# Gate weights in row blocks on two queues, six gate steps abreast, one transpose a tile

## The chip, the cores and the metric

The kernel runs on one core of a Trainium2 chip. Its five engines run side by side and wait for each other through semaphores: TensorE (PE, matmuls; its weight loads are listed as PEld), VectorE (DVE), ScalarE (ACT), GpSimd (POOL) and SyncE (SP, which here only issues DMAs; ACT and POOL issue some too). Matmuls write PSUM, a small memory that ACT and DVE must empty; everything else lies in SBUF, which has 128 partitions. The metric is device time of one execution in microseconds, as the median of three runs.

## The reference

The input x has 2048 tokens of 448 features. It is normalised to xn and goes through a linear recurrence with complex diagonal coefficients (an S5 layer) and, on the other side, through a gated feed-forward block; the two results are multiplied and x is added.

```python
def _B_ref(x, w_gate, w_up, w_down):
    g = jnp.einsum("bsd,df->bsf", x, w_gate)      # 448 -> 1792
    u = jnp.einsum("bsd,df->bsf", x, w_up)
    h = _sigmoid(g) * u
    return jnp.einsum("bsf,fd->bsd", h, w_down)   # 1792 -> 448

xn = _layernorm(x)
s = _A_ref(xn, ...)      # h[t] = Lam_bar * h[t-1] + B_bar xn[t];  2 Re(C h) + xn * Dskip
return x + s * _silu(_B_ref(xn, B_w_gate, B_w_up, B_w_down))
```

Weights, x and the result are bf16.

## The kernel before

**Tiling.** The tokens are cut into 16 tiles of 128 and 4 chunks of 512 (4 tiles). Features lie on partitions for the matmuls, so each tile of xn is transposed into `xnT`. For chunk 0 PE transposes (`pe_transpose`, L511) and ACT and DVE copy the result out of PSUM; for chunks 1 to 3 SP issues DMA transposes (`dma_transpose`, L533), two for a tile: one of four blocks of 128 columns and one of three.

448 is seven times 64. The gate and up weights `wG` and `wU` are therefore held as 7 slots of 64 rows on each half of the partitions: the lower 64 partitions hold the first 896 of the 1792 columns, the upper 64 the other 896. One gate or up step (`gu_mm`, L720) is one block m of 128 columns of each half; it makes 7 pairs of 64-row matmuls (L730, L731), and the two of a pair run side by side on the two halves of the PE array. A chunk has 7 gate and 7 up steps. `xnT` has seven slots too. Slot s of it holds features 64 s to 64 s + 127 (the last wraps round), so its lower half goes with weight slot s and its upper half with weight slot s + 1.

**PSUM.** There are three slots `gu` of two banks each, and two single banks `acc`. A step fills one `gu` slot with 2 x 512 columns. After a gate step ACT takes Tanh of it (`gu_evac`, L748; sigmoid is made from Tanh) and after an up step DVE multiplies (L751). In chunk 0 the gate steps come first, then all up steps. Gate step 3 of chunk 0 uses the two `acc` banks (L743).

**Order.** Every operation is entered with `add` into a plan (class `Plan`). PE's operations keep the order in which they are entered, and so do all DMAs of one queue; ACT, DVE and POOL are ordered by a planner from costs and due times that are written in the code. The `land` arguments are such times; they delay nothing on the chip. At the very start DVE too keeps the entered order (`pl.seq`). Eight semaphores serve the DMAs of SP and ACT in turn, so a DMA is issued only after the eighth before it has landed.

**The start.** SP and ACT load x tiles 0 to 3, then the gate weights in column blocks (L361, L392 to L397): m 0, 1 of the lower half on SP (224 KB) and of the upper half on ACT, then m 2, 3 and m 4 to 6 of the lower half on SP with x tiles 4 to 7 between them, and m 2 to 6 of the upper half in one piece on ACT (560 KB). Four up blocks and `dbc` follow on SP (L412 to L416), then the transposes of B (`b_load`), the tile transposes of chunk 1, `wd`, C (`c_load`), and x tiles 8 to 15 (L1050).

PE first runs matmuls on zeros (`warm_mm`), transposes tiles 0 and 1, and then runs `columns` (L556): small matmuls that turn three rows of parameters (`vrow`, loaded by POOL's queue into `hF`) into columns. From these POOL makes the decay and the angle, and `tables` (L591) makes cosine and sine tables; its first product, iota times angle (L596), is made by ACT. Then PE runs

```python
gu_mm(0, "g", 0, slots0[0], 0, 1, True)       # L1015: step 0, tile 0
gu_mm(0, "g", 0, slots0[0], 1, 2, False)      # step 0, tile 1
gu_mm(0, "g", 1, slots0[1], 0, 2, False)      # step 1, tiles 0, 1
pe_transpose(2, one_bank(0, "DVE"))
pe_transpose(3, one_bank(1, "DVE"))
```

then tiles 2 and 3 of steps 0 and 1, then the steps 2 to 6 with all four tiles, the seven up steps, the products with B (`b_phase`, L777), and so on chunk by chunk, with the down products (L930) and the output products (L959) of earlier chunks between. The recurrence itself is a scan on DVE (L869, L901); its result `hT` (L886, L916) feeds L959.

`norm` (L482) writes xn into one of 8 buffers of 512 columns (the last 64 repeat the first 64, copied by POOL at L493), `skip_row` (L496) makes xn times Dskip into `xd`.

Of the kernel before, what the change touches and what calls it, by code (L numbers as in the profile page):

```python
# [18 lines left out]
D = 448  # L19
F = 1792  # L20
P = 128
# [8 lines left out]
HEAD_DMA = 17  # L30
# [216 lines left out]
def kernel(  # L247
# [39 lines left out]
    NXN = 8  # L287
    xn = [sbt(f"xn{i}", [512]) for i in range(NXN)]
    xnT_raw = [sbt(f"xnT{i}", [7 * L]) for i in range(3)]
    xnT = [flat(t[:], 7, L) for t in xnT_raw]  # L290
    hF_raw = [sbt(f"hF{i}", [FT * L]) for i in range(2)]
# [30 lines left out]
    vrow = hF_raw[0][0:3, 0:448]  # L322
# [38 lines left out]
    BLK = {"g": [(0, 2), (2, 7), (2, 4), (4, 7)], "u": [(0, 3), (3, 7)]}  # L361

    def load_w(eng, k, half, b, r=(), rate=105e3, land=0.0):
        m0, m1 = BLK[k][b]
        ps = slice(half * H, half * H + H)
        c0 = half * 896
        load(eng, [("w", k, half, m) for m in range(m0, m1)], H * 7 * (m1 - m0) * P * 2,
             wgt[k][ps, :, m0 * P:m1 * P],
             wsrc[k][:, c0 + m0 * P:c0 + m1 * P].rearrange("(s p) f -> p s f", p=H), cost=0.65, r=r, rate=rate, land=land)

    def load_wd(h):
        fs = slice(h * 7, h * 7 + 7)
        load("SP", ("wd", h), F * D, wd[:, fs, :], B_w_down.rearrange("(ft p) d -> p ft d", p=P)[:, fs, :],
             rate=400e3, land=41.0 + 2.2 * h)
# [17 lines left out]
    load_w("SP", "g", 0, 0, rate=115e3)  # L392
    load_w("ACT", "g", 1, 0, rate=115e3)
    load_w("SP", "g", 0, 2, rate=400e3, land=9.4)
    load_w("ACT", "g", 1, 1, rate=400e3, land=11.8)
    load_x(4, 2, land=10.8)
    load_w("SP", "g", 0, 3, rate=400e3, land=12.4)  # L397
    load_x(6, 2, land=13.4)
# [13 lines left out]
    load_w("SP", "u", 0, 0, rate=400e3, land=14.8)  # L412
    load_w("SP", "u", 1, 0, rate=400e3, land=16.6)
    load("SP", "dbc", P * D * 2, dbc[:], A_Dskip.unsqueeze(0).to_broadcast((P, D)), rate=400e3, land=17.2)
    load_w("SP", "u", 0, 1, rate=400e3, land=19.2)
    load_w("SP", "u", 1, 1, rate=400e3, land=21.2)  # L416

# [64 lines left out]
    def norm(t):  # L482
        b = t % NXN
        if t < TPC:
            add("DVE", 0.42, lambda: V.tensor_scalar(out=xn[b][:, 0:448], in0=x_all[:, t, :],
                                                     scalar1=meanf[:, t, :], scalar2=rsd[:, t, :],
                                                     op0=ALU.subtract, op1=ALU.mult),
                r=[("x", t), ("mf", t), ("rs", t)], w=[("xn", b)])
        else:
# [3 lines left out]
            add("POOL", 0.2, lambda: G.tensor_copy(out=xn[b][:, 448:512], in_=xn[b][:, 0:64]),  # L493
                r=[("xn", b)], w=[("xnw", b)])

    def skip_row(t):  # L496
        b, q = t % NXN, t % NXD
        add("DVE", dve2(448), lambda: V.tensor_tensor(out=xd[q][:], in0=xn[b][:, 0:448], in1=dbc[:], op=ALU.mult),
            r=[("xn", b), "dbc"], w=[("xd", q)])
# [11 lines left out]
    def pe_transpose(t, parts):  # L511
        b, js = t % NXN, slice(t * P, t * P + P)
# [5 lines left out]
        def f():  # L518
            for s in range(6):
                T.transpose(tp[s], xn[b][:, s * H:s * H + P], ident[:, :])  # L520
            T.transpose(tp[6][0:H, :], xn[b][:, 384:448], ident[:, :])
            T.transpose(tp[6][H:P, :], xn[b][:, 0:H], ident[:, :])
        add("PE", 0.46, f, r=[("xn", b), "ident"], w=[p[2] for p in parts])
# [9 lines left out]
    def dma_transpose(t):  # L533
# [4 lines left out]
        tload([k + ("a",)], xnT[c % 3][:, 0:7:2, js], xn[b][:], P * 1024, r=[("xn", b), ("xnw", b)] + al)  # L538
        tload([k + ("b",)], xnT[c % 3][:, 1:6:2, js], xn[b][:, 64:448], P * 768, r=[("xn", b)] + al)
# [48 lines left out]
    def silu_table():  # L588
        add("ACT", 1.3, lambda: A.preload_act_table_set("silu_and_others"), r=[("sd", t) for t in range(4)] + [("xnT", 0, 2, "a")], w=["silutab"])

    def tables():  # L591
        turn = C("turn")
        for pt in range(4):
            vk, nk = ("v", pt), ("nu", pt)
            v, nu = v_t[:, pt, :], nu_t[:, pt, :]
            add("ACT", 0.61, lambda v=v, pt=pt: A.activation(v, iota[:, 0:NTAB], ACT.Copy, scale=turn[:, pt:pt + 1]),  # L596
                r=[("wv", 0), "turn", "silutab"], w=[vk])
# [28 lines left out]
        gate([("vrow", q) for q in range(3)], [("hF", 0, m) for m in range(7)])  # L626
# [38 lines left out]
    def b_load():  # L665
        for i, m in enumerate((A_B_re, A_B_im)):
            tload([("bT", i)], bT[:, 0:3, i, :], m[:, 0:384], D * 768, land=24.0 + 1.4 * i)
            tload([("bT3", i)], bT[:, 3:4, i, :], m[:, 320:448], D * 256, land=24.4 + 1.8 * i)
# [10 lines left out]
    def c_load():  # L679
        for i, m in enumerate((A_C_re, A_C_im)):  # L680
            tload([("rC", i)], rawC[:, i, 0:3, :], m[:, 0:384], D * 768, land=44.6 + 2.5 * i)
            tload([("rC3", i)], rawC[:, i, 3:4, :], m[:, 320:448], D * 256, land=45.4 + 2.4 * i)
# [37 lines left out]
    def gu_mm(c, k, m, a, lo, hi, first):  # L720
        x = xnT[c % 3]
        bank, keys = ([gu[a][:, 0, :], gu[a][:, 1, :]], [("gu", a)]) if a is not None else (
            [acc[0][:], acc[1][:]], [("acc", 0), ("acc", 1)])
# [4 lines left out]
        def f():  # L728
            for s in range(7):
                T.matmul(bank[0][:, ts], lhsT=w_[0:H, s, ms], rhs=x[0:H, s, ts], start=(s == 0), stop=(s == 6))  # L730
                T.matmul(bank[1][:, ts], lhsT=w_[H:P, (s + 1) % 7, ms], rhs=x[H:P, s, ts],  # L731
                         start=(s == 0), stop=(s == 6))
# [319 lines left out]
    for i in range(4, 13):  # L1052
        gu_step(0, i)
# [82 lines left out]
```

## Time and profile before

| | |
|---|---|
| median of three runs | 185.8 us (185.35 to 186.23) |
| the profiled execution | 186.07 us |
| its span, first to last instruction | 184.3 us |
| granted TensorE clock | 1.00 |
| DVE busy, 40 to 140 us | 97.6 of 100 us |
| read from HBM, written | 6.77 MB, 1.84 MB |

A line of the order of time reads: start, duration, engine, line, operation, what it writes and reads, the shape, the count, and in brackets how long the engine stood idle before it and what ended that. A line of the waits reads: who waited for whom, total time, number of times, longest. In the lines by stretches of time the figures are the busy time of PE, PEld, DVE, ACT and POOL with their counts, then the granted clock, the busy share of the DMA engines, and GB/s. Matmuls overlap, so a busy PE is not a PE at full rate; the starts of successive matmuls tell the rate.

DMAs are told by the time from issue to landing:

```profile
wU<-in_B_w_up_dram SPq DMA_DIRECT2D x2, 448.0 KB, 10.9
...
wG<-in_B_w_gate_dram ACTq DMA_DIRECT2D x1, 560.0 KB, 9.9
wG<-in_B_w_gate_dram SPq DMA_DIRECT2D x2, 224.0 KB, 6.6
...
xnT<-xn SPq DMA_TRANSPOSE x24, 2.4
...
wG<-in_B_w_gate_dram ACTq DMA_DIRECT2D x1, 224.0 KB, 5.5
```

### The profile page before, as it was taken

The numbers are of one execution on the slowest core, as the hardware profiler recorded it, in microseconds if no ns is written. First come the engines' busy times: TensorE is split into PE (matmuls) and PEld (weight loads), VectorE is DVE, ScalarE is ACT, GpSimd is POOL, SyncE is SP. The second block draws the span as 40 slices with busy tenths as digits, with TensorE's granted clock in tenths as the row PEclk, the third lists the DMA queues.
The fourth block names the chain that finished last, engine by engine and source line by source line (L and its number), as shares of the span: only waits on it lengthen the run. The fifth ranks groups of instructions, "written<-read, shape, count | busy, mean of one in ns | idle before, by whom it ended". The sixth has DMA issues, their size and how long they took to land.

```text
span 184.3 us, 3593 instructions
## 1 busy us (share of the span) xinstructions
PE 177.8 (96%) x1395; PEld 88.9 (48%) x1402; DVE 166.1 (90%) x296; ACT 95.7 (52%) x155; POOL 32.5 (18%) x95
## 2 busy tenths in 40 slices
PE   7899999999999999999999999999999999999992
PEld 2664455474554444454554444454555444455551
DVE  3856999599998989999999999999999998999963
ACT  3666999877699897666130452439120523411100
POOL 7355328000047247710000000000000000000000
PEclk9999999999999999999999999999999999999999
DMA  5999994479910340243000000002000000001120
GB/s 139 249 201 211 154 188 88 84 204 279 251 38 20 80 82 21 50 82 71 0 2 0 28 1 0 4 0 75 0 4 0 25 25 5 27 0 50 56 96 28
DMA packets 29826, 13.44 MB, mean 73 GB/s; under 512 B 19760, under 2 KB 29808, under 8 KB 29808
## 3 DMA queue, kind: packets, MB, share of 16 engines
q1 hardware_dynamic: 28496, 12.16, 30.8%
q10 hardware_dynamic: 1216, 1.03, 2.4%
q8 instruction: 11, 0.18, 0.4%
q14 instruction: 7, 0.06, 0.1%
q0 software_dynamic: 96, 0.00, 0.0%
HBM read 6.77 MB, written 1.84 MB: 47 GB/s over the span
## 4 chain that ended last, share of the span: by engine, by line
PE 86%; DMA 7%; ACT 2%; DVE 2%; issue 1%; SPq 1%; DVEq 0%
PE gu L730 39%; PE gu L930 14%; PE acc L959 11%; PE acc L930 9%; PE gu L802 8%; DMA x_all<-in_A_x_dram 7%; PE gu L788 2%; PE acc L805 2%; PE gu L731 1%; ACT hT L596 1%; DVE bst L428 1%; SPq L354 1%; ACT xn L490 1%; ACT hF L748 0%; DVE o_t L975 0%
## 5 line engine op out<-in xcount | busy, mean ns | idle before, releaser
L730 PE MATMUL gu<-xnT,wU 64*128 64x512 bf16 x196 | 45.9, 376 | 0.3 <-ACT hF L748 0.3
L731 PE MATMUL gu<-xnT,wU 64*128 64x512 bf16 x196 | 45.9, 376 | 0.0
L731 PE MATMUL gu<-xnT,wG 64*128 64x512 bf16 (+2 forms) x238 | 44.8, 332 | 0.1
L730 PE MATMUL gu<-xnT,wG 64*128 64x512 bf16 (+2 forms) x238 | 44.8, 332 | 0.1
L748 ACT ACTIVATE sig<-gu 128x1024 f32<-128x1024 f32 x21 | 21.3, 1021 | 23.0 <-PE gu L731 23.0
L930 PEld LDWEIGHTS <-hF 128*128 128x128 bf16 x224 | 21.9, 98 | 20.7 <-issue 0.2
L730 PEld LDWEIGHTS <-wG 64*128 64x128 bf16 x245 | 21.3, 94 | 16.1
L730 PEld LDWEIGHTS <-wU 64*128 64x128 bf16 x196 | 18.4, 94 | 21.7
L751 DVE SCALAR_TENSOR_TENSOR hF<-sig,gu 128x1024 bf16<-128x1024 f32 x21 | 25.5, 1214 | 2.9 <-PE gu L731 2.5
L930 PE MATMUL gu<-wd,hF 128*128 128x448 bf16 x140 | 28.0, 352 | 0.0
L731 PEld LDWEIGHTS <-wG 64*128 64x128 bf16 x245 | 21.2, 94 | 4.4 <-DMA wG<-in_B_w_gate_dram 0.4
L869 DVE TENSOR_TENSOR_SCAN wv<-c_r,st,z 128x512 bf16<-128x512 f32 x18 | 22.9, 1275 | 0.0
L959 PE MATMUL acc<-cT,hT 128*128 128x448 bf16 (+1 forms) x112 | 22.6, 346 | 0.0
L936 ACT ACTIVATE g_t<-gu 128x448 bf16<-128x448 f32 x10 | 5.4, 541 | 28.0 <-PE gu L930 18.9
L731 PEld LDWEIGHTS <-wU 64*128 64x128 bf16 x196 | 18.2, 94 | 1.1 <-issue 1.0
L816 ACT CAST bus<-gu 128x1024 bf16<-128x1024 f32 x12 | 12.0, 1011 | 12.8 <-PE gu L788 12.3
L930 PE MATMUL acc<-wd,hF 128*128 128x448 bf16 x84 | 16.9, 352 | 0.0
L959 PEld LDWEIGHTS <-hT 128*128 128x128 bf16 x119 | 11.5, 98 | 10.1 <-issue 0.4
L802 PE MATMUL gu<-xnT,bT 128*128 128x512 bf16 x65 | 15.3, 379 | 0.4
L428 DVE BATCH_NORM_STATS2 bst<-x_all 128x6 f32<-128x448 bf16 x12 | 7.0, 613 | 5.1 <-DMA x_all<-in_A_x_dram 5.1
L822 ACT CAST bus<-acc 64x256 bf16<-64x256 f32 (+1 forms) x24 | 8.7, 369 | 4.8 <-PE acc L805 4.5
L971 DVE TENSOR_TENSOR o_t<-acc,xd 128x448 bf16<-128x448 f32 (+1 forms) x16 | 9.6, 601 | 1.5 <-PE acc L959 1.4
(146 smaller groups left out, 241.9 us busy)
## 6 DMA issues: line engine op xcount, KB each, us to landing
out_dram<-o_t SPq DMA_DIRECT2D x15, 112.0 KB, 1.7
wd<-in_B_w_down_dram SPq DMA_DIRECT2D x2, 784.0 KB, 5.7
wU<-in_B_w_up_dram SPq DMA_DIRECT2D x2, 448.0 KB, 10.9
x_all<-in_A_x_dram SPq DMA_DIRECT2D x2, 448.0 KB, 4.9
wU<-in_B_w_up_dram SPq DMA_DIRECT2D x2, 336.0 KB, 11.6
wG<-in_B_w_gate_dram ACTq DMA_DIRECT2D x1, 560.0 KB, 9.9
wG<-in_B_w_gate_dram SPq DMA_DIRECT2D x2, 224.0 KB, 6.6
x_all<-in_A_x_dram SPq DMA_DIRECT2D x2, 224.0 KB, 10.2
```

The source lines that it names most:

```text
L428: add("DVE", 0.6, lambda: V.bn_stats(out=bst[b][:], in_=x_all[:, t, :]), r=[("x", t)] + ([("xnT", 0, 3, "a")] if 3 < t < 8 else []), w=[(" ...
L730: T.matmul(bank[0][:, ts], lhsT=w_[0:H, s, ms], rhs=x[0:H, s, ts], start=(s == 0), stop=(s == 6))
L731: T.matmul(bank[1][:, ts], lhsT=w_[H:P, (s + 1) % 7, ms], rhs=x[H:P, s, ts], start=(s == 0), stop=(s == 6))
L748: add("ACT", act(1024), lambda: A.activation(th, gu[a][:], ACT.Tanh, scale=0.5), r=[("gu", a)], w=[tk])
L751: add("DVE", dve1(1024), lambda: V.scalar_tensor_tensor(out=ho, in0=th, scalar=1.0, in1=gu[a][:], op0=ALU.add, op1=ALU.mult), r=[("gu", a) ...
L802: T.matmul(gu[slots[pt]][:, i, :], lhsT=bT[:, kt, i, pt * P:pt * P + P], rhs=x[:, 2 * kt, :], start=(first and kt == 0), stop=(not first a ...
L816: add("ACT", act(1024), lambda: A.copy(out=bus[u][:], in_=gu[slots[pt]][:]), r=key(pt), w=[("bus", u)])
L822: add("ACT", 0.36, lambda ns=ns, d=d, q=q, l=l, i=i: A.copy(out=bus[u][d, l, ns], in_=acc[a3[i]][q, 0:256]), r=[("acc", a3[i])] + ([("bus" ...
L869: dve(1.194, lambda k=k: V.tensor_tensor_scan(out=wv[:, k, :], data0=rb, data1=z[:, k, :], initial=(st[pt][:, k, :] if c else 0.0), op0=AL ...
L930: T.matmul(d, lhsT=hF[c % 2][:, m, h, js], rhs=wd[:, ft, :], start=(ft == 0), stop=(ft == FT - 1))
L959: T.matmul(y, lhsT=hT[c % 2][:, hm, js], rhs=cT[:, cm, c0:c1], start=(i == 0 and not on_pe), stop=(i == 6))
L971: add("DVE", dve1(n), lambda od=od, y=y, c0=c0, c1=c1: V.tensor_tensor(out=od, in0=y, in1=xq[:, c0:c1], op=ALU.add), r=[key, ("xd", q)], w ...
```

## The change

The gate weights are loaded in blocks of whole row slots, (0, 1, 2), (3, 4) and (5, 6), all 896 columns of a half at once: the lower half on SP, the upper half on ACT, three each. `xnT` gets another order of slots (`SL`), so that both matmuls of a pair use the same weight slot. Six gate steps of chunk 0 on tiles 0 and 1 advance together: all six on slots 0 and 1 (tile 0, then tile 1), then on slot 2, then on slots 3 and 4, then on 5 and 6; two steps share one `gu` slot. Tiles 2 and 3 of the six steps follow, and step 6 as before. ACT's Tanh takes two steps for two tiles at a time. `columns` comes after slots 3 and 4. Its rows `vrow` lie in `wU` now, so the first up block is issued after it. x tiles 4 to 7 come as one load, x tiles 8 to 15 are issued after the transposes of B. A tile of chunks 1 to 3 is transposed by one DMA of seven blocks; its xn is 896 columns wide (the row twice), and POOL copies 448 columns instead of 64. There are 4 such buffers; chunk 0 uses `xd` instead. The first product of the tables is made by POOL instead of ACT.

```diff
-    NXN = 8
-    xn = [sbt(f"xn{i}", [512]) for i in range(NXN)]
+    NXN = 4
+    xn = [sbt(f"xn{i}", [2 * D]) for i in range(NXN)]
+    SL = [4 * s % 7 for s in range(7)]
-    vrow = hF_raw[0][0:3, 0:448]
+    vrow = wgt["u"][0:3, 0, 0:448]
...
-    load_w("SP", "g", 0, 0, rate=115e3)
-    load_w("ACT", "g", 1, 0, rate=115e3)
-    load_w("SP", "g", 0, 2, rate=400e3, land=9.4)
-    load_w("ACT", "g", 1, 1, rate=400e3, land=11.8)
-    load_x(4, 2, land=10.8)
-    load_w("SP", "g", 0, 3, rate=400e3, land=12.4)
-    load_x(6, 2, land=13.4)
+    for b, land in ((0, 6.2), (1, 7.8), (2, 9.4)):
+        load_w("SP", "g", 0, b, land)
+        load_w("ACT", "g", 1, b, land)
+    load_x(4, 4, rate=400e3, land=11.5)
...
-            add("POOL", 0.2, lambda: G.tensor_copy(out=xn[b][:, 448:512], in_=xn[b][:, 0:64]),
+            add("POOL", 0.5, lambda: G.tensor_copy(out=xn[b][:, D:2 * D], in_=xn[b][:, 0:D]),
...
-        tload([k + ("a",)], xnT[c % 3][:, 0:7:2, js], xn[b][:], P * 1024, r=[("xn", b), ("xnw", b)] + al)
-        tload([k + ("b",)], xnT[c % 3][:, 1:6:2, js], xn[b][:, 64:448], P * 768, r=[("xn", b)] + al)
+        tload([k + ("a",), k + ("b",)], xnT[c % 3][:, :, js], xn[b][:], P * 1792, r=[("xn", b), ("xnw", b)] + al)
...
-            add("ACT", 0.61, lambda v=v, pt=pt: A.activation(v, iota[:, 0:NTAB], ACT.Copy, scale=turn[:, pt:pt + 1]),
-                r=[("wv", 0), "turn", "silutab"], w=[vk])
+            add("POOL", 0.8, lambda v=v, pt=pt: G.tensor_scalar(out=v, in0=iota[:, 0:NTAB], scalar1=turn[:, pt:pt + 1],
+                                                                scalar2=None, op0=ALU.mult),
+                r=[("wv", 0), "turn"], w=[vk])
...
+    def gu_part(c, k, m, dst, key, lo, hi, s0, s1, opens, first):
...
+            for s in range(s0, s1):
+                u = (s + 6) % 7
+                T.matmul(dst[0], lhsT=w_[0:H, s, ms], rhs=x[0:H, SL[s], ts], start=(s == 0 and opens), stop=(s == 6),
+                         skip_group_check=not opens or s1 < 7)
+                T.matmul(dst[1], lhsT=w_[H:P, s, ms], rhs=x[H:P, SL[u], ts], start=(s == 0 and opens), stop=(s == 6),
+                         skip_group_check=not opens or s1 < 7)
...
+    def two_steps(i, a, lo):
+        ts = slice(lo * P, lo * P + 256)
+        add("ACT", act(1024), lambda: A.activation(hF[1][:, 2 * i:2 * i + 2, :, ts],
+                                                  gu[a][:].rearrange("p h (m t) -> p m h t", m=2), ACT.Tanh, scale=0.5),
+            r=[("gu", a), "silutab"], w=[("hF", 1, 2 * i), ("hF", 1, 2 * i + 1)])
+
+    def pair_part(m, lo, hi, s0, s1, a, opens, first=False):
+        o = 256 * (m % 2) + P * (lo % 2)
+        n = (hi - lo) * P
+        gu_part(0, "g", m, [gu[a][:, i, o:o + n] for i in range(2)], [("gu", a)], lo, hi, s0, s1, opens, first)
...
+    for t in range(2):
+        for m in range(6):
+            pair_part(m, t, t + 1, 0, 2, slots0[m // 2], t == 0 and m % 2 == 0, t == 0 and m == 0)
+    for s0, s1 in ((2, 3), (3, 5)):
+        for m in range(6):
+            pair_part(m, 0, 2, s0, s1, slots0[m // 2], False)
     columns(0)
+    load_u("SP", 0, 0, 14.0, w=[("vrow", k) for k in range(3)])
+    load_u("SP", 1, 0, 15.0)
+    load_u("SP", 0, 1, 17.0)
+    load_u("SP", 1, 1, 19.0)
...
+    for m in range(2):
+        pair_part(m, 0, 2, 5, 7, slots0[m // 2], False)
     pe_transpose(2, one_bank(0, "DVE"))
     pe_transpose(3, one_bank(1, "DVE"))
     silu_table()
     pl.seq = False
...
+    two_steps(0, slots0[0], 0)
+    for m in range(2, 6):
+        pair_part(m, 0, 2, 5, 7, slots0[m // 2], False, m == 2)
+        if m % 2:
+            two_steps(m // 2, slots0[m // 2], 0)
+    for m in range(6):
+        pair_part(m, 2, 4, 0, 7, slots0[m // 2], True)
+        if m % 2:
+            two_steps(m // 2, slots0[m // 2], 2)
     b_load()
+    load_x(8, 4, rate=400e3, land=24.0)
+    load_x(12, 4, rate=400e3, land=25.0)
```

## The prediction

> **What bounds the kernel now.** I read the table of engines first, then the chain of waits, then TensorE's (PE's) own waits, and last the order of time from 5 to 21 us on PE.
>
> ```profile
> span 184.3 us, 3593 instructions
> ...
> PE 177.8 (96%) x1395; PEld 88.9 (48%) x1402; DVE 166.1 (90%) x296; ACT 95.7 (52%) x155; POOL 32.5 (18%) x95
> ...
> PE 86%; DMA 7%; ACT 2%; DVE 2%; issue 1%; SPq 1%; DVEq 0%
> ...
> PE acc L561 <- DMA hF<-in_A_Lambda_re_dram: 0.5, 1, 0.5
> ...
> PEld L731 <- DMA wG<-in_B_w_gate_dram: 0.4, 1, 0.4
> ...
> PE gu L730 <- ACT hF L748: 0.3, 1, 0.3
> ```
>
> PE holds 86% of the chain that ended last, and its list of waits is short. From the first up step at 20.39 to 179.9 us I found no gap on PE over 0.25 us. So the kernel is PE's work laid end to end, and its time moves only if the point moves at which PE begins the up steps, or if a new hole opens. DVE is 98% busy from 40 to 140 us, but it finishes ahead of PE's need: the last part of hT of chunk 3 (L886) ends at 170.4 and its first reader (L959) starts at 172.5; for the earlier chunks the lead is 4.9 us or more. A shift of about one us is inside that.
>
> So the change is priced between 7.00 us, where PE takes up `columns`, and 20.39 us, where the first up step starts.
>
> ```profile
> 7.00 0.21 PE L561 MATMUL acc<-ident,hF 3*128 3x3 bf16 x3 [0.54 <-DMA hF<-in_A_Lambda_re_dram]
> ...
> 7.26 0.23 PE L730 MATMUL gu<-xnT,wG 64*128 64x128 bf16 x1
> ...
> 8.71 0.27 PE L730 MATMUL gu<-xnT,wG 64*128 64x256 bf16 x1
> ...
> 10.32 0.21 PE L730 MATMUL gu<-xnT,wG 64*128 64x128 bf16 x1
> ...
> 11.88 0.38 PE L730 MATMUL gu<-xnT,wG 64*128 64x512 bf16 x1
> 12.35 0.39 PE L731 MATMUL gu<-xnT,wG 64*128 64x512 bf16 x1
> ...
> 20.39 0.37 PE L730 MATMUL gu<-xnT,wU 64*128 64x512 bf16 x1 [0.32 <-ACT hF L748]
> ```
>
> These 13.39 us hold the gate steps, the transposes of tiles 2 and 3, and three holes: 0.17 before 10.32 (the copy of tile 3), 0.26 at 11.88 (a gate block not landed), 0.48 before 20.39 (a PSUM slot that ACT had not emptied). Together 0.91 us. The rate of the loads is in these stretches (the last column is GB/s):
>
> ```profile
> 3.50:4.50 1.00, 1.00 (x4) 0.35 (x3) 0.96 (x4) 0.30 (x1) 0.94 (x8) 1.00 0.65 146
> 4.50:5.50 1.00, 0.66 (x9) 0.43 (x7) 0.89 (x5) 0.30 (x1) 0.19 (x1) 1.00 1.03 274
> 5.50:6.50 1.00, 0.96 (x13) 0.56 (x10) 0.86 (x3) 0.59 (x2) 0.00 (x0) 1.00 1.13 298
> ...
> 7.00:8.00 1.00, 1.00 (x33) 0.96 (x34) 0.78 (x3) 0.55 (x3) 0.39 (x2) 1.00 1.07 209
> ...
> 40.00:42.00 2.00, 2.00 (x21) 0.85 (x18) 1.90 (x3) 1.14 (x2) 0.00 (x0) 1.00 1.08 375
> ```
>
> While blocks for both partition halves are in flight (4.5 to 6.5) the queues move 274 to 298 GB/s; with one half alone (7 to 8, ACT's 560 KB block) 209; wd, which spans all 128 partitions, 375.
>
> **Part 1, the start of the gate steps.** The first block is now three row slots for each half: 64 x 3 x 1792 B = 344 KB, 688 KB for the pair. All six steps need both, so PE starts when the later one has landed; call this T0. I count 40 KB of the x tiles as still to come at 3.5 us. Late end: at the rates of before, 146 + 274 + 298 = 718 KB are moved at 6.5, so the mean arrival of 728 KB is about 6.55. The lag of the last part behind the mean comes from the old first pair: 459 + 40 KB are through at 4.5 + (499 - 146)/274 = 5.8, but ACT's block, issued at 1.70, took 5.5 and landed at 7.2, a lag of 1.4. That gives T0 = 7.95. Early end: T0 can't be before tile 0's xnT is copied, 5.85 + 0.36 = 6.2. I take 6.8: 330 GB/s from 3.5 on (between 298 for pieces of 512 B and 375 for wd's of 896 B; the new pieces are 1792 B, and the weak second at 3.5, with a DMA share of 0.65, has fewer pieces to describe), 728/330 = 2.2, so 5.7, and a lag of 1.1.
>
> **Part 2, PE's work from T0 to the first up step.** A pair of 128 columns costs 0.0557 (28 of them from 10.32 to 11.88), of 256 columns 0.11, of 512 columns 0.2155. Slots 0, 1 on tiles 0 and 1 apart: 24 x 0.0557 = 1.34. Slot 2: 6 x 0.11 = 0.66. Slots 3, 4: 1.32. `columns`, moved in here: 0.26. Slots 5, 6 of steps 0, 1: 0.44. Transposes of tiles 2, 3 with their transitions, 8.82 to 10.32 less the hole of 0.17: 1.33. Slots 5, 6 of steps 2 to 5: 0.88. Tiles 2, 3: 42 x 0.11 = 4.62. Step 6: 7 x 0.2155 = 1.51. Sum 12.36. One hole is new: the copy of tile 3 (0.62 on DVE, after transposes and tile 2's copy) ends about 2.1 after the transposes start, PE is there after 1.33 + 0.88 less transitions: 0.0 to 0.3, I take 0.15. So the first up step starts at 6.8 + 12.5 = 19.3 instead of 20.39: a gain of 1.1. Bounds: 6.2 + 12.36 = 18.6 (gain 1.8) and 7.95 + 12.66 = 20.6 (a loss of 0.2).
>
> The cover of this sum: the second pair (459 KB) must land by T0 + 2.0, the third by T0 + 3.6. At 330 GB/s they come 1.4 and 2.8 after T0, so they cost nothing; without that cover see the first rival. The three PSUM slots now hold two steps each for half the tokens. ACT empties slot 0 in 1.02 (the row of Tanh) while PE has 1.33 + 0.88 of other work, slots 1 and 2 have 1.5 and 3 us more: nothing. The 0.48 hole goes, as four 0.62 copies of the tables leave ACT. Against a gain stands the third load on ACT's queue: it waits for an x tile that landed by 3.9, ahead of ACT's first Sqrt at 4.05; that Sqrt may slip 0 to 0.3, covered by 0.5 between tile 0's copy and T0.
>
> **Part 3, what moves behind it.** The four up blocks wait for `columns`, since vrow now lies in wU; PE reads it at about 10.1. SP stands until then with everything behind it. The up load then runs 11.5 to 11.5 + 1606/222 = 18.7 (222 GB/s was its rate at 18 to 20). Steps 0 to 2 have theirs at 14.6 + 1.4 = 16.0 against 19.3 needed, the rest at 20.1 against 23.8. Hidden by 3 us. The tables' products on POOL: between 0.57 (IOTA on the same 513 elements) and 1.05 (its pow) each, done by 17 us; before, ACT gave the last at 22.5. Nothing for PE. POOL's copy of the row grows from 64 to 448 columns; 0.24 and, for 192 columns, 0.35 are in the trace, so about 0.57, twelve times: POOL is 18% busy.
>
> One transpose a tile: the four-block one took 1.21 to issue and the three-block one 1.25, so width did not set it. Four at 1.25 (I take this) or, at the other end, 2.5 for both together. They come after x of chunks 2, 3: the B transposes end some 4.5 after the last up block, as before, at 23.7; x takes 918/375 = 2.5; then 4 x 1.25 to 4 x 2.5, and 2.4 to landing: 33.6 to 38.6. PE wants tiles 6 and 7 at 38.2 - 1.1 = 37.1. So 0 or, at worst, 1.5; I take 0. Later loads of wd and C only come earlier.
>
> **Sum.** 184.3 - 1.1 = 183.2 of span. The profiled execution took 186.07, 1.77 more than its span and 0.27 over the median 185.8; 184.97 in its terms is 184.7 against the median. Its own range by the bounds is 184.0 to 186.0.
>
> **Rivals.** *The halves don't add up.* With row blocks the two queues move no more than one half's 209 GB/s. Then the first pair is through at 3.5 + 728/209 = 7.0, plus 1.4 is 8.4; the second lands at 10.6, the third at 12.8, and after the third PE still has 0.44 + 1.33 + 0.88 + 0.15 + 4.62 + 1.51 = 8.95: up steps from 21.8, a loss of 1.4, 187.2. It decides from a third pair landing after 20.39 - 8.95 = 11.4. For it: over 11 to 19 us, where single halves follow each other, the rate stays near 222. Against it: 274 to 298 with both halves in flight. *Late but without holes.* The lag of 1.4 stays and nothing else: 20.5, 185.9, no change that can be told. For it: the landing of the old pair. *The transposes eat it.* Chunk 1 waits 1.5: 186.2; against it, the two equal issue times.
>
> On the first rival the Trainium skill takes a side. "SBUF — State Buffer", section "Can I just issue two DMAs to hit both halves?", says no: two transfers at once, one to each partition half, were only 6% faster than one. The 298 against 209 GB/s here disagree with it, by 43%; by the rule (1.06 x 209 = 222 GB/s) the third pair would land at about 12.4 and the kernel would be some 1 us slower, by the measured rows it is 1.1 faster. I go by the rows.
>
> **How the numbers follow.** A measurement can tell about 0.5%, 0.9 us, from no change. Forecast 0.55, of it 0.50 faster and 0.05 within; halves 0.23, of it 0.21 slower, 0.02 within; late start 0.14 (0.02 faster, 0.11 within, 0.01 slower); transposes 0.08 (0.05 within, 0.03 slower). Together faster 0.52, same 0.23, slower 0.25. The range goes from 183.8 to 187.0: it takes in both ends of the forecast, the late start and the transposes, and most of the halves.
>
> **What would show it.** Right: the first gate matmul near 6.8, no gap over 0.3 on PE up to 19.3, 300 GB/s or more from 4.5 to 8.5, first up step near 19.3, span near 183.2, nothing new in PE's waits later. The first rival: PE waiting for wG at 9 to 13 us and 210 to 230 GB/s there. The second: first gate matmul at 7.9. The third: PE waiting for xnT near 36. I would be wrong in kind if PE waited for DVE, or for wU, after 20 us.

## The result, and the profile after

| | before | after |
|---|---|---|
| median of the paired runs, us | 186.01 (185.35 to 186.63) | 194.02 (192.32 to 195.03) |
| profiled execution, its span, us | 186.07, 184.3 | 195.03, 193.2 |
| granted clock over the span | 1.0 | 0.979 |
| first gate matmul on both halves, us | 7.26 | 9.21 |
| first up step, us | 20.39 | 24.29 |

The changed kernel is slower: ratio 1.042, interval 1.038 to 1.047. The forecast was 184.7, and its range ended at 187.0. Runs of one kernel differ here in good part by how many windows of 3.41 us of PE's clock were halved (clock 1.0, 0.99 or 0.98 over the span, some 1.7 us each), so clocks are named below where a median mixes them.

The page of the changed kernel: span, table of engines, the clock in 40 slices of 4.83 us (tenths), and the chain that ended last.

```profile
span 193.2 us, 3668 instructions
...
PE 180.9 (94%) x1433; PEld 95.7 (50%) x1440; DVE 168.2 (87%) x296; ACT 93.3 (48%) x150; POOL 49.6 (26%) x99
...
PEclk9759999999999999999999999999999999999998
...
PE 65%; POOL 14%; DMA 7%; ACT 5%; SPq 4%; issue 2%; DVE 2%; ACTq 0%; POOLq 0%; DVEq 0%
```

Before, the chain was PE at 86% and no POOL at all; now POOL holds 14% and PE 65%. The clock has a dent in slices 2 and 3. PE's list of waits (engine, line, releaser, total, times, longest), without the one of 1.2 at the start that both kernels have:

```profile
PE acc L942 <- ACT bus L834: 3.5, 1, 3.5
...
PE gu L730 <- DMA wG<-in_B_w_gate_dram: 1.2, 1, 1.2
PE gu L728 <- DMA wG<-in_B_w_gate_dram: 1.2, 1, 1.2
PE gu L728 <- DVE hF L763: 0.8, 1, 0.8
```

Each is one place. In order of time they are these.

**The head.** Windows of 1 us of the changed kernel (last three columns: granted clock, DMA share, GB/s), then PE in order of time.

```profile
3.00:4.00 1.00, 1.00 (x4) 0.30 (x3) 0.81 (x3) 0.00 (x0) 0.93 (x8) 1.00 0.71 178
4.00:5.00 1.00, 0.90 (x5) 0.34 (x3) 1.00 (x5) 0.53 (x2) 0.64 (x4) 1.00 0.68 192
5.00:6.00 1.00, 0.83 (x11) 0.62 (x11) 0.66 (x4) 0.33 (x2) 0.00 (x0) 1.00 0.98 325
6.00:7.00 1.00, 0.61 (x8) 0.28 (x5) 0.36 (x1) 0.67 (x2) 0.00 (x0) 1.00 1.07 334
7.00:8.00 1.00, 0.24 (x1) 0.10 (x1) 0.84 (x2) 0.13 (x1) 0.00 (x0) 0.83 1.04 255
8.00:9.00 1.00, 0.05 (x1) 0.00 (x0) 0.97 (x5) 0.30 (x1) 0.18 (x1) 0.50 1.07 267
...
13.00:14.00 1.00, 1.00 (x14) 1.00 (x11) 0.00 (x0) 0.00 (x0) 0.00 (x0) 0.50 0.00 0
14.00:15.00 1.00, 1.00 (x17) 0.93 (x13) 0.00 (x0) 0.00 (x0) 0.00 (x0) 0.75 0.00 0
```

```profile
7.76 0.29 PE L728 MATMUL gu<-xnT,wG 64*128 64x128 bf16 x1 [1.15 <-DMA wG<-in_B_w_gate_dram]
9.21 0.29 PE L730 MATMUL gu<-xnT,wG 64*128 64x128 bf16 x1 [1.16 <-DMA wG<-in_B_w_gate_dram]
...
9.29 0.31 PE L730 MATMUL gu<-xnT,wG 64*128 64x128 bf16 x1
...
9.40 0.31 PE L730 MATMUL gu<-xnT,wG 64*128 64x128 bf16 x1
...
24.29 0.38 PE L728 MATMUL gu<-xnT,wU 64*128 64x512 bf16 x1
```

PE stood from 6.6 to 9.2 for the first block: SP's half came at 7.72, the last of ACT's 16 parts at 9.16, though its 15th was there at 8.00. From 7.66 to 14.49 us, two windows of 3.41, the clock was halved: pairs of 128 columns follow 0.107 apart, where they took 0.0557 before. The loads ran dry: from 13 to 15 us nothing moved.

**The tables.** POOL, then DVE, of the changed kernel in order of time (start, duration, idle time before in brackets).

```profile
17.94 5.22 POOL L595 TENSOR_SCALAR hT<-wv,c_turn 128x513 f32<-128x513 f32 x3
...
24.52 1.07 POOL L469 TENSOR_TENSOR sdb<-veb,halfc 128x2 bf16<-128x2 bf16 x1
25.59 1.57 POOL L595 TENSOR_SCALAR hT<-wv,c_turn 128x513 f32<-128x513 f32 x1
```

```profile
27.20 0.43 DVE L598 TENSOR_SCALAR hT<-hT 128x513 f32<-128x513 f32 x1 [0.31 <-POOL hT L595]
27.54 1.05 DVE L600 SCALAR_TENSOR_TENSOR hT<-hT,hT 128x513 f32<-128x513 f32 x1
28.51 2.34 DVE L763 SCALAR_TENSOR_TENSOR hF<-hF,gu 128x1024 bf16<-128x1024 bf16 x2
```

A product takes 1.57 to 1.83 us on POOL (three in 5.22) against 0.71 on ACT before. The last one ends at 27.2; DVE's order has the fourth table ahead of the first products of hF, so those start at 28.5, and PE, which had filled the three PSUM slots, stood 0.95 at 28.6 (the 0.8 of the list) and 0.3 at 36.

**C.** SP's queue, then the ACT line behind which PE waited.

```profile
4.08 0.56 SPq L355 DMA_DIRECT2D x_all<-in_A_x_dram  x1
15.40 2.65 SPq L355 DMA_DIRECT2D wU<-in_B_w_up_dram  x4
18.10 0.63 SPq L355 DMA_DIRECT2D dbc<-in_A_Dskip_dram  x1
18.77 6.25 SPq L383 DMA_TRANSPOSE bT<-in_A_B_re_dram  x2
...
40.44 5.90 SPq L383 DMA_TRANSPOSE xnT<-in_A_C_re_dram  x2
46.38 3.80 SPq L383 DMA_TRANSPOSE xnT<-in_A_C_im_dram  x2
```

```profile
51.51 0.67 ACT L693 ACTIVATE ctmp<-xnT,c_n2i 128x448 f32<-128x448 bf16 x1 [3.79 <-DMA xnT<-in_A_C_im_dram]
```

SP issued nothing from 4.6 to 15.4, because the up load has to wait until `columns` has read vrow out of wU. B, x and C came after it; C's transposes started at 40.44 (38.42 before) and landed at 48 to 52 (45.6 to 48.7 before). ACT has one fixed order, and it puts the products with C (L693) ahead of the copies (L834) that empty the accumulators PE needs at 49.9. That order comes from C's due times, which the change moved from 44.6 and 45.4 to 38.6 and 39.4 (`c_load`; those lines are not among the ones shown with the change). ACT stood 3.79, PE 3.5.

The sum on PE: first up step +3.90, 0.95 and 0.3 for the tables, 3.5 for C: 8.65 of the 8.9 us by which the span grew.

### The profile page after: what moved, and what is told of

It is laid out like the page before. It is cut to its first block, busy times and chain, and to the rows that moved or that the text cites. A ratio compares the mean times of both kernels' runs of the same rounds, so it can differ in the third digit from the quotient of the medians.

```text
span 193.2 us, 3668 instructions
## 1 busy us (share of the span) xinstructions
PE 180.9 (94%) x1433; PEld 95.7 (50%) x1440; DVE 168.2 (87%) x296; ACT 93.3 (48%) x150; POOL 49.6 (26%) x99
## 3 DMA queue, kind: packets, MB, share of 16 engines
q10 hardware_dynamic: 784, 1.03, 1.9%
## 4 chain that ended last, share of the span: by engine, by line
PE 65%; POOL 14%; DMA 7%; ACT 5%; SPq 4%; issue 2%; DVE 2%; ACTq 0%; POOLq 0%; DVEq 0%
PE gu L728 29%; PE gu L942 11%; PE acc L971 11%; PE acc L942 5%; PE gu L814 4%; DMA wG<-in_B_w_gate_dram 4%; POOL hT L595 4%; PE gu L730 3%; SPq L383 3%; DMA xnT<-in_A_C_im_dram 3%; POOL rsd L475 2%; POOL sdb L469 2%; ACT ctmp L693 1%; POOL xn L490 1%; ACT bus L828 1%
## 5 line engine op out<-in xcount | busy, mean ns | idle before, releaser
L728 PE MATMUL gu<-xnT,wG 64*128 64x512 bf16 (+2 forms) x264 | 48.9, 337 | 1.2 <-DMA wG<-in_B_w_gate_dram 1.2
L730 PE MATMUL gu<-xnT,wG 64*128 64x512 bf16 (+2 forms) x264 | 48.7, 337 | 1.2 <-DMA wG<-in_B_w_gate_dram 1.2
L760 ACT ACTIVATE sig<-gu 128x1024 f32<-128x1024 f32 x21 | 21.4, 1022 | 30.3 <-PE gu L730 25.0
L728 PEld LDWEIGHTS <-wG 64*128 64x128 bf16 x264 | 25.6, 101 | 17.9 <-DMA wG<-in_B_w_gate_dram 1.3
L728 PEld LDWEIGHTS <-wU 64*128 64x128 bf16 x196 | 18.4, 94 | 21.5
L730 PEld LDWEIGHTS <-wG 64*128 64x128 bf16 x264 | 25.6, 101 | 1.3 <-DMA wG<-in_B_w_gate_dram 1.3
L490 POOL COPY xn<-xn 128x448 bf16<-128x448 bf16 x12 | 8.8, 751 | 35.7 <-ACT xn L487 35.6
L971 PEld LDWEIGHTS <-hT 128*128 128x128 bf16 x119 | 11.5, 98 | 10.1 <-issue 0.4
L487 ACT ACTIVATE xn<-x_all,nmr,rsd 128x448 bf16<-128x448 bf16 x12 | 8.7, 755 | 5.3 <-issue 1.3
```

Of the source, the lines that this page charges most:

```text
L487: add("ACT", 0.65, lambda: A.activation(xn[b][:, 0:448], x_all[:, t, :], ACT.Identity, bias=nmr[:, t, :], scale=rsd[:, t, :]), r=[("x", t) ...
L490: add("POOL", 0.5, lambda: G.tensor_copy(out=xn[b][:, D:2 * D], in_=xn[b][:, 0:D]), r=[("xn", b)], w=[("xnw", b)])
L728: T.matmul(dst[0], lhsT=w_[0:H, s, ms], rhs=x[0:H, SL[s], ts], start=(s == 0 and opens), stop=(s == 6), skip_group_check=not opens or s1 < 7)
L730: T.matmul(dst[1], lhsT=w_[H:P, s, ms], rhs=x[H:P, SL[u], ts], start=(s == 0 and opens), stop=(s == 6), skip_group_check=not opens or s1 < 7)
L760: add("ACT", act(1024), lambda: A.activation(th, gu[a][:], ACT.Tanh, scale=0.5), r=[("gu", a)], w=[tk])
L971: T.matmul(y, lhsT=hT[c % 2][:, hm, js], rhs=cT[:, cm, c0:c1], start=(i == 0 and not on_pe), stop=(i == 6))
```

## The experiments

Each kernel is the changed one with the edit shown. Ratios are to the kernel before on the same chip, with 95% intervals.

**One cause at a time.** First, twelve matmuls of 512 columns on zeros before the first gate step, so that PE does not idle.

```
+    def keep_warm():
+        for _ in range(12):
+            T.matmul(gu[slots0[0]][:, 0, :], lhsT=warm[:, 0:P], rhs=warm[:, 0:512], start=True, stop=True)
+    add("PE", 0.0, keep_warm, r=["warm"], w=[("gu", slots0[0])])
```

> The changed kernel with 12 matmuls of 512 columns on zeros between the transposes of tiles 0, 1 and the gate steps, so that TensorE is not idle from 6.4 to 9.2 us. Theory (the idle wait for the first gate blocks halves TensorE's clock from 7.7 to 14.5 us): granted clock 1.0 throughout, the gate work from 9.2 to 14.5 us takes half its 5.3 us, so about 2.6 us less, 191.4. Rival (the loads alone set that stage, the clock costs nothing): 194.0 whatever the clock.

191.6 us, 1.031 (1.023 to 1.039); clock 0.997 or more in three of four runs. The clock is held, but twelve were too many: the first gate step started at 9.78, though both halves of the block were there at 7.7, and the first up step came at 22.33. PE's wait behind C (1.7) and the table hole (0.8) stay. So the expected 191.4 nearly came, but by another sum: of the 3.7 us between the profiled spans 1.96 is the head, where 2.6 was expected, and 1.8 the shorter wait behind C.

Second, vrow back in hF, so that the up load waits for nothing.

```
-    vrow = wgt["u"][0:3, 0, 0:448]
+    vrow = hF_raw[0][0:3, 0:448]
-    load_u("SP", 0, 0, 14.0, w=[("vrow", k) for k in range(3)])
+    load_u("SP", 0, 0, 14.0)
+        gate([("vrow", q) for q in range(3)], [("hF", 0, m) for m in range(7)])
```

> The changed kernel with the three parameter rows back in hF, so that the up loads don't wait for columns. Theory (the up loads' wait until 15.4 us pushes B, x, the transposes and C back by some 8 us, and ScalarE then stands 3.8 us before the C scaling): up loads issued by 6 us, C landed by 45 us instead of 52, TensorE's 3.5 us wait for ScalarE at 50 us gone, 190.5. Rival (C is late for its own place in SP's queue): C still lands near 50 us and the time stays at 194.

187.3 us, 1.0106 (1.0064 to 1.0148), clock 0.997 or more in six of seven runs. The up load is issued at 5.05, C lands by 44.1, and ACT's hole is gone. PE's waits of this kernel, without the common one:

```profile
PE gu L730 <- DVE hF L765: 0.8, 1, 0.8
PE gu L730 <- DMA wG<-in_B_w_gate_dram: 0.7, 1, 0.7
```

What is left is the table hole and the wait for the first block. With the full clock the gate steps start at 7.94 and the first up step at 20.50: the head is level with before's 20.39 and not ahead of it. This is the largest of the single effects, 6.7 us of the 8 by the medians, 7.7 between the two profiled executions. Only 3.5 of that is C; the rest goes with the clock (2.6) and the earlier landing of the first block in this profile (1.3). The edit touches neither, so that these two come from it is not shown: of the later kernels with rows apart some have the halved clock again.

Third, the table products back on ACT.

```
-            add("POOL", 0.8, lambda v=v, pt=pt: G.tensor_scalar(out=v, in0=iota[:, 0:NTAB], scalar1=turn[:, pt:pt + 1], ...
+            add("ACT", 0.61, lambda v=v, pt=pt: A.activation(v, iota[:, 0:NTAB], ACT.Copy, scale=turn[:, pt:pt + 1]), ...
```

> The changed kernel with the first product of the tables back on ScalarE. Theory (GpSimd's four products of 1.6 to 1.9 us each hold back its pow for chunk 1 and so VectorE's first up products): the 0.95 us hole at 28.6 us goes, 193.0. Rival (hidden): 194.0. The clock and the wait at 50 us stay in both.

191.35 us, 1.026 (1.020 to 1.033). The wait for hF is gone, the one for C stays (3.6), and the clock was halved once in three of four runs; the run at clock 1.0 took 189.4. It is faster than the expected 193.0, but not by the tables: of the 3.5 us between the profiled spans 2.25 is the head (first gate step 7.91, one halved window instead of two), and 1.25 is left for the tables.

Fourth, only ACT's order: C's due times, which the planner orders by, 10 us later.

```
-            tload([("rC", i)], ..., land=38.6 + 2.5 * i)
+            tload([("rC", i)], ..., land=48.6 + 2.5 * i)
-            tload([("rC3", i)], ..., land=39.4 + 2.4 * i)
+            tload([("rC3", i)], ..., land=49.4 + 2.4 * i)
```

> The changed kernel with the planner's due times of the C loads 10 us later (38.6 to 48.6 and so on); the loads themselves keep their place. Theory (C's lateness costs only because ScalarE's order, made from the old due times, puts the C scaling before the emptying of b_phase 1): the C scaling comes behind it, TensorE's 3.5 us wait goes, 190.5. Rival (C itself is needed then): 194 or more.

190.1 us, 1.017 (1.009 to 1.025): the wait for C is gone, the one for hF stays. The runs order themselves by the clock: 192.3 at 0.98, 190.2 and 190.0 at 0.991, 187.6 at 1.0. In the profiled one the first block came as late as 9.89 and the first up step at 25.17, 0.9 later than in the changed kernel; with 3.5 less behind it the span should be 190.6, and it is 190.5.

**Two together, and the head.** Rows apart and tables on ACT, the second and third edit:

> The changed kernel with both the parameter rows back in hF and the tables' first product back on ScalarE. Theory (what is left after the rows are apart is the 0.95 us hole before an up product and 0.3 at b_phase 0, both from GpSimd's four products, 6.8 us together): no hole over 0.3 us on TensorE after the first gate matmul, 187.3 - 1.25 = 186.1. Rival (the hole comes from VectorE's own backlog after the late statistics of chunk 1): it stays, 187.3.

188.6 us, 1.0117 (1.0082 to 1.0152), 187.2 and 187.6 where the clock was 1.0. In the profiled run it was halved from 8.82 to 12.23, and a new wait of 0.6 for ACT's copies shows: the planner wrote another order, and C's products stand ahead of them again. The expected 186.1 was missed, at the full clock too. On top of that, the first block cut to two slots:

```
-    BLK = {"g": [(0, 3), (3, 5), (5, 7)]}
+    BLK = {"g": [(0, 2), (2, 5), (5, 7)]}
```

> As the run before, and the gate blocks cut at slots 2 and 5 instead of 3 and 5, so that the first pair is 459 KB as in the kernel before instead of 688 KB. Theory (the first block's size and the lag of its last part set when the gate steps start; 7.1 us instead of 7.9, then 12.5 us of work to the first up step): first up step at 19.6, 185.3, faster than before by 0.4 us. Rival (the next pair is then missed: 688 KB more by 8.4 us): a hole of 0.5 to 1 us before slot 2, 186.1 again.

And the same cut alone on the changed kernel:

> The changed kernel with the gate blocks cut at slots 2 and 5 and nothing else. Theory (the clock is halved because TensorE idles too long before the first gate matmul): the first matmul near 7.1 to 7.5 us, granted clock 1.0 in most executions, 190 to 191. Rival (the clock falls whatever the start): clock 0.98 to 0.99, 193.

189.0 us, 1.0147 (1.0125 to 1.0169), and 189.4 us, 1.0158 (1.0111 to 1.0206). The gate steps start at 7.36 and 7.35, half a us earlier, and PE stands instead for the second block, which lands at 9.9 to 10.1: first up step 21.4 and 21.1. The start was won and lost again 2.5 us later. In the first of the two PE also waited for ACT behind C, which adds to its time:

```profile
PE acc L943 <- ACT bus L835: 1.6, 1, 1.6
```

The cut alone brings the changed kernel from 194.0 to 189.4, since with it the clock stayed at 0.996 or more in three of four runs and C was not late. Its lines of the up load and of ACT's first product with C, to be read beside those of the changed kernel (15.40, and a stand of 3.79):

```profile
12.25 2.65 SPq L355 DMA_DIRECT2D wU<-in_B_w_up_dram  x4
```

```profile
44.88 0.67 ACT L693 ACTIVATE ctmp<-xnT,c_n2i 128x448 f32<-128x448 bf16 x1 [0.30 <-DMA xnT<-in_A_C_im_dram]
```

ACT's order is the same there, and vrow still lies in wU. PE read it 3.2 us earlier (11.99 against 15.15), and PE's wait of 3.5 is gone.

Then the fifth kernel with all six gate blocks on SP's queue:

```
-        load_w("ACT", "g", 1, b, land)
+        load_w("SP", "g", 1, b, land)
```

> As e5, but all six gate blocks are issued on SP, lower and upper half in turn. Theory (two queues keep both halves in flight, 325 to 350 GB/s from 5 to 7 us): on one queue the halves come one after the other at some 210 to 230 GB/s, the third pair lands near 12.5 us instead of 11.5, holes on TensorE, 1 us more than e5. Rival (two transfers to two halves gain nothing over one after the other): the same landing times and the same time as e5.

189.2 us, 1.0169 (1.0145 to 1.0193). The time is no measure of the queues, since ACT's order opened a longer wait behind C than in the fifth kernel (0.6), and the clock was halved behind it, from 47.91:

```profile
PE acc L943 <- ACT bus L835: 2.3, 1, 2.3
```

The loads can be compared. The windows of 5 to 8 us, and for two queues of 10 to 11, first with two queues (the kernel with rows apart), then with one:

```profile
5.00:6.00 1.00, 1.00 (x10) 0.64 (x9) 0.68 (x3) 0.09 (x1) 0.01 (x1) 1.00 1.01 354
6.00:7.00 1.00, 0.94 (x11) 0.60 (x11) 0.36 (x1) 0.60 (x2) 0.00 (x0) 1.00 1.08 330
7.00:8.00 1.00, 0.29 (x3) 0.16 (x5) 0.51 (x2) 0.46 (x1) 0.00 (x0) 1.00 1.09 244
...
10.00:11.00 1.00, 1.00 (x23) 1.00 (x20) 0.40 (x1) 1.00 (x1) 0.00 (x0) 1.00 1.09 256
```

```profile
5.00:6.00 1.00, 1.00 (x10) 0.62 (x9) 0.69 (x3) 0.10 (x1) 0.02 (x1) 1.00 1.08 275
6.00:7.00 1.00, 1.00 (x10) 0.69 (x11) 0.36 (x1) 0.59 (x1) 0.00 (x0) 1.00 1.07 228
7.00:8.00 1.00, 0.42 (x4) 0.17 (x4) 0.20 (x1) 0.48 (x1) 0.00 (x0) 1.00 1.07 246
```

Two queues are faster for two us, 354 and 330 against 275 and 228 GB/s; from 7 us on both move about 245. Over 5 to 7 us the eleven profiles with two queues and a first block of three slots have 288 to 361 in the mean, the one profile with one queue 252. But the first pair landed at 8.05 with one queue and at 7.7 to 9.9 with two, the third at 11.72 against 11.0 to 12.4. So two queues buy nothing that lands earlier, neither the first block nor the whole gate weight, as far as one profile with one queue can tell. Where the clock is full and nothing else holds PE up, the first up step is the later of two sums: the first gate step plus 12.55, or the landing of the third pair plus 8.9 (8.95 in the prediction). The third pair decides with rows apart (11.59 and 20.50) and with one queue (11.72 and 20.64). In the kernel of the next part it was there at 11.16, and the first gate step decides: 8.27 and 20.82.

**All three undone.** Rows apart, tables on ACT, and C's due times 6 us later, which is where the kernel before had them.

```
-            tload([("rC", i)], ..., land=38.6 + 2.5 * i)
+            tload([("rC", i)], ..., land=44.6 + 2.5 * i)
-            tload([("rC3", i)], ..., land=39.4 + 2.4 * i)
+            tload([("rC3", i)], ..., land=45.4 + 2.4 * i)
```

> The changed kernel with vrow back in hF, the four table products back on ACT, and the due time by which ACT's order is written moved 6 us later for C. Theory (the loss is three holes behind a head that gains nothing): no wait of PE over 0.5 us after the first up step; where the clock is granted in full, gate start 7.9, third pair 11.6, first up step 20.5, and 186.6 (187.2, the best of rows apart and tables on ACT, less its hole of 0.6); 188.2 where one window of 3.4 us is halved; median 186.6 to 187.6, so within 1% of before and not faster. Rival (something else of the change costs time all along the stages): 188 or more even in runs at clock 1.0. Rival (the forecast's head was right once the rest is mended): first up step at 19.3 to 19.8 and 185 or less.

188.0 us, 1.0125 (1.0082 to 1.0168). No wait behind C over 0.2, none for hF at 28 us, but a new one of 1.0 for hF at 62 us: DVE stood 2.0 at 49 us for ACT's C products, which are later now, and is behind at the next chunk. The theory's "no wait over 0.5" was wrong. The same with two DMA transposes a tile and POOL's narrow copy:

```
-        tload([k + ("a",), k + ("b",)], xnT[c % 3][:, :, js], xn[b][:], P * 1792, ...
+        tload([k + ("a",)], xnT[c % 3][:, 0:4, js], xn[b][:, 0:512], P * 1024, ...
+        tload([k + ("b",)], xnT[c % 3][:, 4:7, js], xn[b][:, 64:448], P * 768, ...
```

> As the kernel with the three parts undone, and also two DMA transposes a tile again (four and three blocks) with POOL's copy of 64 columns instead of 448. Theory (the single transpose is hidden both ways): the same time within 0.5%, and PE waits for xnT nowhere. Rival (the wide copy on POOL or the single wide transpose costs time): 1 us or more faster. Rival (the single transpose helps): 1 us or more slower.

188.5 us, 1.0128 (1.0084 to 1.0172): no difference that shows (one run at clock 1.0, 187.3, beside 187.3 to 188.2; the other three had a window halved). SP issued the eight transposes of chunk 1 in 11.5 us instead of four in 7.0, and nobody waited for xnT. And the kernel with the three parts undone with four keep-warm matmuls, where the first run had twelve:

```
+        for _ in range(4):
```

> As the kernel with the three parts undone, and four matmuls of 512 columns on zeros between tile 1's transposes and the first gate step, some 1.1 us at the granted clock of 0.9 or 1.0, which end before the first gate block lands at 7.9. Theory (PE standing idle while it waits for the first pair lets the clock fall): clock 0.995 or more in all runs, and a narrower spread than without, 186.4 to 187.2. Rival (the clock falls by chance or for another cause): as many runs at 0.99 or below as without.

187.7 us, 1.0089 (1.0055 to 1.0123); clock 0.997 or more in all six runs, against two of six at 0.991 without. Then an attempt to use the wait, again in the kernel with the three parts undone: first block of two slots, transposes of tiles 2 and 3 moved into it.

```
+    pe_transpose(2, one_bank(0, "DVE"))
+    pe_transpose(3, one_bank(1, "DVE"))
     for s0, s1 in ((2, 3), (3, 5)):
```

> As the kernel with the three parts undone, and the first block two slots instead of three, statistics of tile 2 ahead of tile 1's copy on DVE, and the transposes of tiles 2 and 3 between slots 0, 1 and slot 2, where PE would wait for the second pair. Theory (the head is bounded by the landing of the blocks; what is put into the wait comes off behind it): gate start 7.35, slots 0, 1 until 8.7, transposes until 10.2, slots 2 to 4 until 12.2, then columns 0.26, and 7.45 of work from the third pair on (8.95 less the transposes and their hole): first up step 19.9 to 20.1, 185.4 to 186.0, no difference from before that can be told, 0.5 to 1 under the kernel with the three parts undone. Rival (the third pair decides with the whole 8.95 behind it): first up step at 20.5 or later.

187.8 us, 1.010 (1.007 to 1.013), first up step 20.96. The expected 20.0 was missed: tile 2's statistics, put ahead on DVE, made tile 1's copy late (0.55), the transposes waited 0.25 for their input, and a PSUM slot cost 0.41. The rival's number (20.5 or later) came, by other waits than it named.

**Is there a rest?** Two smaller shifts of C's due time, with rows apart, tables on ACT and the four matmuls; and the first of them again with the fill in place of the four matmuls, without the statistics moved.

```
-            tload([("rC", i)], ..., land=44.6 + 2.5 * i)
+            tload([("rC", i)], ..., land=41.6 + 2.5 * i)
```

(41.6 and 42.4 in the first and third, 42.6 and 43.4 in the second.)

> Rows apart, tables on ACT, the four short matmuls that hold the clock, and C's due time 3 us later instead of 6. Theory (nothing is lost but the head and the holes seen): no wait of PE over 0.5 us after the first up step, first up step 20.5 to 21.0, 185.9 to 186.5, so 0 to 0.3% above before. Rival (a rest that no hole shows): PE's waits are gone and it still takes 187.2 or more.

> The same with 4 us. Theory: as with 3 us, 185.9 to 186.5, unless the order that comes of it opens the hole at 47 us (0.6) or at 62 us (1.2), which then shows in PE's waits and in the time with its own size. Rival: 187.2 or more without such a hole.

> Rows apart, tables on ACT, C due 3 us later, the first block two slots, the transposes of tiles 2 and 3 between slots 0, 1 and slot 2; DVE's order as in the changed kernel, so tile 1's copy isn't late. Theory: gate start 7.2, slots 0, 1 until 8.6, transposes from 9.2 (tile 2's norm) to 10.6, slots 2 to 4 until 12.7, columns 0.28, slots 5, 6 1.32, a slot wait of 0.4, 6.13 of tiles 2, 3 and step 6: first up step 20.8; with no later hole 186.0 to 186.4. Rival (the fill pays): first up step under 20.2 and below before.

| | us (runs) | ratio, interval | first up step | longest wait after it |
|---|---|---|---|---|
| C 3 us later, warm | 187.6 (12) | 1.0071, 1.0040 to 1.0101 | 21.16 | 0.6 for hF at 63 us |
| C 4 us later, warm | 187.9 (12) | 1.0088, 1.0059 to 1.0117 | 20.34 | 0.9 for hF at 62 us |
| fill, C 3 us later | 188.3 (6) | 1.0111, 1.0064 to 1.0158 | 21.49 | 0.3 for hF at 63 us |

All 30 runs with the four matmuls show a clock of 0.995 or more, and so do the 12 with the fill; of the ten runs of the two kernels with the three parts undone and neither, five are at 0.991 or less. In the kernel with 4 us the head is level with before (20.34 against 20.39), and the time is still 1.5 us of span longer. Two lines of DVE in order of time say where most of it went:

```profile
48.49 0.69 DVE L697 SCALAR_TENSOR_TENSOR cT<-xnT,c_c,ctmp 128x448 bf16<-128x448 bf16 x1 [2.18 <-ACT ctmp L694]
...
61.74 1.19 DVE L764 SCALAR_TENSOR_TENSOR hF<-sig,gu 128x1024 bf16<-128x1024 f32 x1
```

DVE stood 2.18 for ACT's C products, and PE stood for the hF of 61.74 (0.9 in its list, 1.03 of time). Another 0.3 lies at 45 us. So a wait shows for some 1.35 of the 1.5. The same sum fits the other two, each 2.0 us of span over the kernel before: 0.8 of head and holes of 0.3 at 32, 0.4 at 46 and 0.75 at 64 us in the first; 1.1 of head, 0.4 at 46 and 0.5 at 64 in the third. So, to some 0.2 us, no cost is left that is spread over the stages. The hoped-for end, a mended kernel at 185.9 to 186.5, was not reached; whether a due time exists that opens neither the hole at 47 nor the one at 62 was not settled. The change also moved the due times of B (24.0 to 21.5) and wd (41.0 to 34.0), and no run put those back. No version tried beats the kernel before.

## Why the prediction was wrong, by its own steps

- **"I take 6.8" for the first gate step: too early, and nearer to its late end of 7.95.** In the eight kernels that keep the three-slot block on two queues and start it as it lands it came at 7.8 to 8.4, in a ninth at 9.94, in the changed kernel at 9.21. Two terms were off. The rate of 330 GB/s held from 5 to 7 us only (325 and 334); from 3 to 5 it was 178 and 192, so that the 728 KB counted are through at 6.4, not 5.7. And the lag of the slowest part behind that was 2.8, not 1.1 (1.5 to 3.5 in the other nine). The bytes moved were not the first block's alone: parts of SP's second block landed from 7.11 on, ahead of the last of ACT's first.
- **The clock was not a term at all.** The steps were priced at 0.0557 a pair, as in the kernel before, whose PE stood 0.8 at most between 6 us and the up steps. The change makes all work of tiles 0 and 1 wait for one block of 688 KB, PE stands, and the work of 9.21 to 14.49 then ran at half speed: 5.28 / 2 = 2.6 us.
- **The work from the start to the first up step, 12.36 + 0.15: right.** At full clock 12.56 (7.94 to 20.50) and 12.54 (7.80 to 20.34). The 0.48 hole went, as said.
- **"The second pair ... the third ... cost nothing": right by nothing.** PE needs the third pair at its start plus 3.6; in the kernel with rows apart that is 11.54, and it landed at 11.59. The point from which the first rival decides, 11.4, was passed in most profiles with the three-slot blocks, but not in all (11.0 to 12.4). Its time, 187.2, is what the kernel with rows apart took (187.3), but that is luck: 1.25 of that kernel's excess of 1.6 is the tables. A row given for this rival was misread, too: before, 11 to 19 us moved 208 GB/s, not near 222.
- **The rule weighed against it.** The 298 GB/s I went by is real and was even exceeded, at 354. The rule of the Trainium skill, "SBUF — State Buffer", section "Can I just issue two DMAs to hit both halves?", that two transfers to the two halves serialize, does not describe these two us, in which two queues moved 14 to 43% more than one (288 to 361 against 252 GB/s). For what landed when, it would have been the better guide.
- **The tables on POOL, "between 0.57 ... and 1.05 ... Nothing for PE": wrong in size, and the cover was gone.** 1.57 to 1.83 each, started at 17.9, done at 27.2 instead of 17; 1.25 us on PE. The sign named for being wrong in kind came here: PE waited for DVE after 20 us. Neither neighbour bounded it: IOTA reads no tensor, and the pow works on a few elements of each row.
- **"Later loads of wd and C only come earlier": wrong, and the largest single wait.** SP's stand until `columns` was seen and held against the up load only (hidden, as said: PE never waits for wU). The same delay went on to B, x and C. That ACT's order is written by C's due time, 6 us earlier in this change, was in the diff and was not followed: 3.5 us. This step stands on the first two. The forecast had PE read vrow at about 10.1; the late block and the halved clock made it 15.15. With the small first block alone it was 11.99, C was issued at 34.86 (38.42 before), earlier as the forecast said, and PE's wait was gone in the same order of ACT. With twelve matmuls it was 13.19, and the wait 1.7. So at 10.1 the wait would most likely not have shown; that was not run.
- **One transpose a tile, cost 0: right.** Undone, it changes nothing.

Over the predicted span of 183.2 the measured 193.2 lies by 10.0: the start 2.4, the clock 2.6, the tables 1.25, C 3.5, together 9.75. No rival had the clock or C in it, and C's 3.5 follows from the first two.

## What to carry to other kernels

Where early work is cut so that it needs a little of a whole load instead of all of a small one, its end is set by the last byte and the work left behind that byte; count that before counting the start. A buffer borrowed by an early load delays the queue it sits in, and the delay must be followed to the last transfer of that queue and to the engine orders that were written for the old landing times. On TensorE a wait of some 2 us ahead of its work cost twice here, once as idle time and once in the clock that followed.

## What the hardware showed that was not expected

- **The clock.** Halved stretches are multiples of 3.41 us: 7.66 to 14.49 in the changed kernel, 7.83 to 11.24 with the tables on ACT, 8.70 to 15.53 with C's due time later, and, for the kernel with rows apart and tables on ACT, these windows:

```profile
8.00:9.00 1.00, 0.83 (x21) 0.70 (x23) 0.97 (x5) 0.30 (x1) 0.19 (x1) 0.91 1.06 229
9.00:10.00 1.00, 1.00 (x24) 1.00 (x22) 0.88 (x5) 0.77 (x2) 0.33 (x1) 0.50 1.11 236
...
12.00:13.00 1.00, 1.00 (x20) 1.00 (x18) 0.00 (x0) 0.00 (x0) 0.00 (x0) 0.88 1.11 222
```

  PE was 1.00 busy there at a clock of 0.50; the dent follows the wait, it does not lie in it. In the head, the window ahead of a halving had PE busy for 1.60 to 2.19 of its 3.41 us; windows with 2.30 or more were not followed by one. At 48 us, where matmuls fill all 128 rows, one window of 1.16 was followed by a halved one (47.91 to 51.33, with one queue), and six of 1.54 to 1.82 were not. So it is not busy time alone that counts. The Trainium skill, "TensorE: Matmul & The Clock Gate", Part 1, has the half rate, the free-running window of 3413 ns, and a return to half rate after an idle window; the length agrees, but here a window that was idle for 1.2 us of 3.4 was enough.
- **The slowest of 16 parts.** In the changed kernel ACT's first block had 15 of 16 parts at 8.00 and the last at 9.16. What holds that part up was not tried.
- **The fall from 330 to 250 GB/s** at 7 us, with both halves still in flight, shows in the changed kernel and with rows apart (334 to 255, 330 to 244). With a first block of two slots it comes at 6 us in all four profiles (360 to 235, 329 to 260, 352 to 255, 359 to 219), so it seems to go with the size of the first block and not with the time. Its cause stays open too.
- **A product of 513 float32 elements on POOL**, one input and a scalar for each partition, took 1.57 to 1.83 us, 2.2 to 2.6 times the 0.71 of the same product on ACT before.
